# The first exponential's column moves into the identity's tile, and every later tile begins 1408 or 1376 bytes higher

## The chip, the cores and the metric

The kernel runs on one core of a Trainium2 chip. Its time is the device time of one execution in microseconds (us), and the figure shown is the median of three runs. Beside the runs stands one profiled execution, which the hardware profiler recorded instruction by instruction. The engines are called as the profile calls them: PE (TensorE's matmuls), PEld (TensorE's loads of the stationary operand), DVE (VectorE), ACT (ScalarE), POOL (GpSimd) and SP (SyncE, which issues nearly all transfers here).

## The reference

The reference computes an attention with a detour over 32 packed queries, and a feed-forward layer behind it, all in float32.

```python
def sm_attn(qq, kk, vv):                      # softmax attention, 8 batches, 8 heads
    s = scale * np.matmul(qq, kk.transpose(0, 1, 3, 2))
    a = np.exp(s - np.max(s, axis=-1, keepdims=True))
    a = a / (np.sum(a, axis=-1, keepdims=True) + 1e-09)
    return np.matmul(a, vv)
p_packed = sm_attn(p, k, v)                   # 32 packed rows from 576 tokens
out = sm_attn(q, p_packed, p_packed)          # 576 tokens from 32 packed rows
x = out.transpose(0, 2, 1, 3).reshape(4608, 512)
h = x @ w_in                                  # 512 -> 2048
g = h * (1.0 / (1.0 + np.exp(-h)))
return g @ w_out                              # 2048 -> 512
```

## The kernel before

The eight batches are worked through one after the other, with the attention of the next one laid between the feed-forward units of the present one. A unit is one batch and one block `f` of 128 of the 2048 hidden columns. For it, line 524 makes the hidden values (the product of the second softmax's shares `a2` with `pw`, which is the packed rows times `w_in`), lines 542 to 545 apply the activation, line 550 makes the remainder of the rounding, and line 560 adds the product with the rows of `w_out` to the sums in PSUM. To keep float32 accuracy on rounded operands, each product is made from three: upper by upper, upper by lower, lower by upper. So there are `g_hi` and `g_lo`, `wo_hi` and `wo_lo`, `pw_hi` and `pw_lo`, `a2_hi` and `a2_lo` (`a_hi` and `a_lo` in the profile).

In both lines the matmul has a stationary operand of 128 columns of 4 bytes (512 bytes in each partition), which PEld loads ahead, and a moving operand that PE streams. In line 560 the stationary operand is a block of `g` and the moving one a row of `w_out`, 512 columns or 2048 bytes. In line 524 the stationary one is a block of `pw` and the moving one is half of `a2`, 288 columns or 1152 bytes. The first few units (`u < WHOLE`) work on unrounded float32 with one product instead of three.

For PE, DVE, ACT and SP the order of the instructions is written out by hand: the string `ORDER` for the first two batches, `step_of` and the loop at the end for the others. Neither reads an address. At the start, POOL makes the identity (`make_identity`, line 112), ACT takes one exponential of its first column into `ready` (line 121), which brings the exponential's table in before it is needed, and PE multiplies the identity by itself (`keep_warm`, line 138, the step `W6`) until the first keys have landed (`k0`, line 144) and the first scores can start (`as0.0`, line 231). The framework finds out which instruction must wait for which from the tiles that they read and write.

Tiles in SBUF are laid out in the order of their pools and of their first use, one behind the other. `const` holds `ident`, `win`, `wo_hi`, `wo_lo`, `rest` and `ready`; behind it come `kvq`, `pw`, `a2p`, `tmp`, `small`, `gp`, `osb`, the staging buffers of the weights (`w_raw`) and, in the same place later, the third buffers of `pw` and `g`. A tile of `const` smaller than 32 bytes takes 32. In the program before, `ident` begins at byte 16512 of each partition, behind the framework's own 16384 + 128 bytes.

Of the kernel before, what the change touches and what calls it, by code (L numbers as in the profile page):

```python
# [9 lines left out]
F32 = mybir.dt.float32  # L10
# [9 lines left out]
P = 128  # L20
# [63 lines left out]
def packed_attention_ffn(ctx: ExitStack, tc: tile.TileContext, pkT, qT, v, w_in, w_out, out):  # L84
# [15 lines left out]
    const = ent(tc.tile_pool(name="const", bufs=1))  # L100
# [7 lines left out]
    ps_acc = ent(tc.tile_pool(name="ps_acc", bufs=2, space=PSUM))  # L108
    ps_two = ent(tc.tile_pool(name="ps_two", bufs=2, space=PSUM))

    ident = const.tile([P, P], F32, name="ident")
    make_identity(nc, ident)
    win = const.tile([P, NF, NI, P], I32, name="win")
    wo_hi = const.tile([P, NF, DM], F32R, name="wo_hi")
# [2 lines left out]
    rest = const.tile([P, NF, 2, 2, REST], F32, name="rest")  # L117
    parts = tc.dram_tile((EARLY, 2, P, 2, DM), F32, name="parts")

    ready = const.tile([P, 1], F32, name="ready")  # L120
    nc.scalar.activation(ready, ident[:, :1], AF.Exp)

    made = {}
# [663 lines left out]
```

## Time and profile before

| | |
|---|---|
| median of 3 runs | 717.23 us (717.07 to 717.65) |
| profiled execution, its own time | 716.94 us |
| its span, first to last instruction | 715.1 us |
| PE busy | 702.2 us, 98% of the span |
| DVE, ACT busy | 332.5 us, 328.7 us |

The span leaves out what lies before the first and behind the last instruction, 1.8 us here. PE's busy time counts a matmul until its end, and the matmuls of a row overlap one another, so the sum over groups is larger than the span and the spacing of starts says more than the durations. In the chain of waits, a piece is a stretch in which one line on one engine set the pace; its length divided by its count is the spacing of that line's matmuls.

### The profile page before, as it was taken

Reading aid. Unit: us, or ns where it says so; the run is one execution under the profiler, and the core shown is the slowest. Engines: PE = TensorE matmul, PEld = TensorE weight load, DVE = VectorE, ACT = ScalarE, POOL = GpSimd, SP = SyncE. Lnnn points to the kernel's source line nnn. Section 1 sums busy time; section 2 is a strip of 40 time slices with the busy share of each in tenths; the row PEclk is TensorE's granted clock in tenths of the full one; section 3 lists DMA queues with packets and bytes.
Section 4 is the critical chain, followed back from the end, with each engine's and each line's share of the span. In section 5 each row is a group of like instructions: output and inputs, shape, how many; then the busy total and the mean of one; then the engine's idle time right before and its main releaser. Section 6 shows DMA issues by size and latency. Waiting matters only on the chain.

```text
span 715.1 us, 12103 instructions
## 1 busy us (share of the span) xinstructions
PE 702.2 (98%) x5060; PEld 563.6 (79%) x5060; DVE 332.5 (46%) x491; ACT 328.7 (46%) x614; POOL 21.0 (3%) x16
## 2 busy tenths in 40 slices
PE   8999999999999999999999999999999999999997
PEld 5647778877778888878888788878878788788885
DVE  4989985944632346332542425432362333622112
ACT  4796858534535325362532625452343533533221
POOL 0202020200000000000000000000000000000000
PEclk9999999999999999999999999999999999999999
DMA  9765654405022130312112122112301210010002
GB/s 361 312 192 217 221 186 173 125 32 192 23 107 81 35 144 1 126 23 89 67 60 82 22 83 74 59 68 45 134 0 68 74 35 1 1 59 1 1 1 73
DMA packets 30869, 65.20 MB, mean 91 GB/s; under 512 B 19296, under 2 KB 19296, under 8 KB 26464
## 3 DMA queue, kind: packets, MB, share of 16 engines
q1 hardware_dynamic: 30720, 64.30, 25.9%
q8 instruction: 40, 0.66, 0.4%
q10 hardware_dynamic: 96, 0.13, 0.1%
q14 instruction: 13, 0.11, 0.0%
HBM read 48.76 MB, written 11.53 MB: 84 GB/s over the span
## 4 chain that ended last, share of the span: by engine, by line
PE 91%; DVE 4%; ACT 2%; DMA 1%; SPq 1%; issue 0%; ACTq 0%; DVEq 0%
PE ps_acc L560 56%; PE ps_two L524 27%; PE ps_two L231 6%; SPq L308 1%; PE ps_two L329 1%; DMA w_raw<-in_w_in 1%; DMA kvq_t<-in_pkT 1%; ACT tm L277 0%; PE ps_acc L231 0%; DVE win L204 0%; DVE mx L267 0%; DVE win L203 0%; PE ps_acc L329 0%; DVE tm L411 0%; DVE tm L434 0%
## 5 line engine op out<-in xcount | busy, mean ns | idle before, releaser
L560 PE MATMUL ps_acc<-wo_hi,g_hi 128*128 128x512 f32 x560 | 225.2, 402 | 0.0
L560 PE MATMUL ps_acc<-wo_hi,g_lo 128*128 128x512 f32 x560 | 221.5, 396 | 0.1
L560 PE MATMUL ps_acc<-wo_lo,g_hi 128*128 128x512 f32 x560 | 221.2, 395 | 0.0
L550 DVE TENSOR_TENSOR g_lo<-g,g_hi 128x512 fp32r<-128x512 f32 x124 | 89.3, 720 | 260.6 <-ACT g_hi L544 260.5
L542 ACT ACTIVATE g<-ps_two 128x512 f32<-128x512 f32 x124 | 74.4, 600 | 270.2 <-PE ps_two L524 241.1
L524 PE MATMUL ps_two<-a_lo,pw_hi 128*128 128x288 f32 x528 | 156.0, 304 | 0.1
L524 PE MATMUL ps_two<-a_hi,pw_hi 128*128 128x288 f32 x496 | 146.3, 295 | 1.0 <-ACT rest L545 1.0
L524 PE MATMUL ps_two<-a_hi,pw_lo 128*128 128x288 f32 x496 | 146.6, 296 | 0.0
L560 PEld LDWEIGHTS ps_acc<-wo_hi,g_hi 128*128 128x128 f32 x560 | 105.1, 188 | 40.1 <-issue 19.4
L560 PEld LDWEIGHTS ps_acc<-wo_hi,g_lo 128*128 128x128 f32 x560 | 105.2, 188 | 26.2 <-DVE g_lo L550 0.8
L560 PEld LDWEIGHTS ps_acc<-wo_lo,g_hi 128*128 128x128 f32 x560 | 105.2, 188 | 19.7
L524 PEld LDWEIGHTS ps_two<-a_lo,pw_hi 128*128 128x128 f32 x528 | 99.4, 189 | 7.4 <-ACT rest L545 0.8
L524 PEld LDWEIGHTS ps_two<-a_hi,pw_hi 128*128 128x128 f32 x496 | 93.1, 188 | 6.1 <-ACT rest L545 1.3
L524 PEld LDWEIGHTS ps_two<-a_hi,pw_lo 128*128 128x128 f32 x496 | 93.2, 188 | 0.0
L544 ACT ACTIVATE g_hi<-ps_two 128x512 fp32r<-128x512 f32 x124 | 73.7, 594 | 8.4 <-PE ps_acc L560 8.2
L492 DVE TENSOR_TENSOR pw_lo<-ps_two,pw_hi 128x1024 fp32r<-128x1024 f32 x31 | 36.8, 1220 | 10.0 <-ACT pw_hi L489 10.0
L489 ACT CAST pw_hi<-ps_two 128x1024 fp32r<-128x1024 f32 x31 | 30.1, 1015 | 16.7 <-PE ps_two L231 16.7
L231 PE MATMUL ps_two<-win,ppT 64*32 64x512 f32 (+1 forms) x560 | 32.7, 559 | 2.5 <-DVE pw_lo L492 1.6
L545 ACT ACTIVATE rest<-ps_two 128x64 f32<-128x64 f32 (+1 forms) x132 | 30.0, 228 | 0.0
L231 PEld LDWEIGHTS ps_two<-win,ppT 64*32 64x32 f32 x560 | 8.2, 105 | 18.0 <-issue 10.4
L542 ACT ACT_TABLE_LOAD x16 | 20.5, 1283 | 2.1 <-PE ps_two L524 1.9
L534 ACT CAST g_hi<-rest 128x512 fp32r<-128x512 f32 x16 | 9.9, 622 | 14.6 <-PE ps_acc L560 14.6
(116 smaller groups left out, 475.7 us busy)
## 6 DMA issues: line engine op xcount, KB each, us to landing
kvq_t<-in_v SPq DMA_DIRECT2D x8, 1280.0 KB, 6.4
kvq_t<-in_pkT SPq DMA_DIRECT2D x7, 1216.0 KB, 6.4
out<-o SPq DMA_DIRECT2D x16, 512.0 KB, 2.8
kvq_t<-in_qT SPq DMA_DIRECT2D x7, 1152.0 KB, 5.3
w_raw<-in_w_in SPq DMA_DIRECT2D x6, 1024.0 KB, 6.6
win<-in_w_out SPq DMA_DIRECT2D x3, 1024.0 KB, 5.5
w_raw<-in_w_out SPq DMA_DIRECT2D x3, 1024.0 KB, 4.7
tm<-tm SPq DMA_DIRECT2D x56, 40.0 KB, 2.0
```

Source lines behind the costliest of these rows:

```text
L231: nc.tensor.matmul(bank(par)[NP * i : NP * i + NP], lhs(r, i), rhs(r, i), start=True, stop=True)
L308: nc.sync.dma_start(self.e1T[NP * at : NP * at + NP, : some.shape[1], i], some)
L329: nc.tensor.matmul(self.ps[NP * i : NP * i + NP, par * D : par * D + D], e, vs[:n, c, h * D : h * D + D], start=(c == 0), stop=(c == 4),)
L489: nc.scalar.copy(self.hi, self.ps[:, :, : self.nf * P])
L492: nc.vector.tensor_tensor(self.lo, self.ps[:, :, : self.nf * P], self.hi.bitcast(F32), ALU.subtract)
L524: nc.tensor.matmul(bank, p[:, par, cols], a[:, par], start=(n == 0), stop=(n == len(todo) - 1))
L534: nc.scalar.copy(g_hi, g)
L542: nc.scalar.activation(g, ps[..., :MAIN], AF.Silu)
L544: nc.scalar.activation(g_hi, ps[..., :MAIN], AF.Silu)
L545: nc.scalar.activation(to, ps[..., MAIN:HS], AF.Silu)
L550: nc.vector.tensor_tensor(g_lo[:, c], g[:, c], g_hi[:, c].bitcast(F32), ALU.subtract)
L560: nc.tensor.matmul(bank, g[:, rows], w[:, at], start=(first and n == 0), stop=(last and n + 1 == len(todo)))
```

## The change

`ident` becomes a tile of 480 columns instead of 128, which is 1408 bytes longer. The program goes on using the first 128 columns under the name `ident`; column 128 is `ready`, and the other 351 are not used. The tile `ready` of its own goes away, with its 32 bytes.

```diff
-    ident = const.tile([P, P], F32, name="ident")
+    ident = const.tile([P, P + 352], F32, name="ident")
+    ready = ident[:, P : P + 1]
+    ident = ident[:, :P]
     make_identity(nc, ident)
 ...
-    ready = const.tile([P, 1], F32, name="ready")
     nc.scalar.activation(ready, ident[:, :1], AF.Exp)
```

No instruction is added or taken away, and no order is changed. `win`, `wo_hi`, `wo_lo` and `rest` begin 1408 bytes higher, and everything behind `const` begins 1376 bytes higher. By the sizes of the tiles, that moves the first bytes so:

| tile | before, modulo 2048 | modulo 512 | modulo 128 | after, modulo 2048 | modulo 512 | modulo 128 |
|---|---|---|---|---|---|---|
| `ident` | 128 | 128 | 0 | 128 | 128 | 0 |
| `win`, `wo_hi`, `wo_lo` (rows of 2048), `rest` | 640 | 128 | 0 | 0 | 0 | 0 |
| `kvq_t`, `pw` (blocks of 512), `tm` | 672 or 1696 | 160 | 32 | 0 or 1024 | 0 | 0 |
| `a2`, eight buffers of 2304, each in halves of 1152 | all different | 32, 160, 288, 416 | 32 | all different | 0, 128, 256, 384 | 0 |
| `g_hi`, `g_lo`, `g` (blocks of 512), `o`, `w_raw` | 1696 | 160 | 32 | 1024 | 0 | 0 |

The first byte of a moving `w_out` row and that of the stationary `g` block beside it differ by 32 bytes modulo 128 before, and by none after. Those of `a2` and `pw` differ by 0 modulo 128 before and after. The highest byte in use goes from 226976 to 228352.

## Prediction

> **What bounds the kernel now.** I read the page first: the engines' busy shares, the granted clock and the chain of waits.
>
> ```profile
> PE 702.2 (98%) x5060; PEld 563.6 (79%) x5060; DVE 332.5 (46%) x491; ACT 328.7 (46%) x614; POOL 21.0 (3%) x16
> PEclk9999999999999999999999999999999999999999
> PE 91%; DVE 4%; ACT 2%; DMA 1%; SPq 1%; issue 0%; ACTq 0%; DVEq 0%
> ```
>
> PE is busy in 98% of the span and is 91% of the chain, at the full granted clock throughout. What an address can change must therefore show in the pace of PE's matmuls; DVE, ACT and the transfers together hold some 7% of the chain. Next come the groups by line and form, for the counts.
>
> ```profile
> L560 PE MATMUL ps_acc<-wo_hi,g_hi 128*128 128x512 f32 x560 | 225.2, 402 | 0.0
> L560 PE MATMUL ps_acc<-wo_hi,g_lo 128*128 128x512 f32 x560 | 221.5, 396 | 0.1
> L560 PE MATMUL ps_acc<-wo_lo,g_hi 128*128 128x512 f32 x560 | 221.2, 395 | 0.0
> L524 PE MATMUL ps_two<-a_lo,pw_hi 128*128 128x288 f32 x528 | 156.0, 304 | 0.1
> L524 PE MATMUL ps_two<-a_hi,pw_hi 128*128 128x288 f32 x496 | 146.3, 295 | 1.0 <-ACT rest L545 1.0
> L524 PE MATMUL ps_two<-a_hi,pw_lo 128*128 128x288 f32 x496 | 146.6, 296 | 0.0
> ```
>
> Line 560 has 3 x 560 = 1680 rounded matmuls of 512 columns. Line 524 has 3 x 496 = 1488 of 288 columns, and 32 of the 528 are the unrounded ones of the first units. PE waits for almost nothing (the last column). The chain in order of time (start, length, what, count) gives the spacing of these matmuls.
>
> ```profile
> 0.74 3.81 DMA kvq_t<-in_pkT
> 52.60 6.78 DMA w_raw<-in_w_in
> ...
> 65.55 3.20 PE ps_two L524 x24
> ...
> 180.41 3.19 PE ps_two L524 x24
> ...
> 362.32 11.19 PE ps_acc L560 x48
> ...
> 531.56 11.19 PE ps_acc L560 x48
> ...
> 652.98 3.19 PE ps_two L524 x24
> 691.26 19.61 PE ps_acc L560 x84
> ```
>
> Line 560: 19.61/84 = 233.5 ns, 11.19/48 = 233.1 ns. Line 524: 3.19/24 = 132.9 ns. The spacing stays the same over 600 us, and it does not depend on what the other engines do, as the view by stretches shows (busy us and counts of PE, PEld, DVE, ACT, POOL, then clock, DMA share, GB/s).
>
> ```profile
> 151.20:154.10 2.90, 2.90 (x13) 2.35 (x14) 2.36 (x2) 1.14 (x2) 0.00 (x0) 1.00 0.02 6
> 362.40:373.40 11.00, 11.00 (x49) 8.82 (x48) 4.52 (x6) 4.55 (x8) 0.00 (x0) 1.00 0.26 97
> 695.00:710.00 15.00, 15.00 (x66) 12.00 (x66) 3.42 (x5) 2.88 (x4) 0.00 (x0) 1.00 0.19 70
> ```
>
> DVE is busy 41% of the second stretch (4.52 of 11.00) and 23% of the last (3.42 of 15.00), and the spacing is 233.1 against 233.5 ns. So traffic of DVE and ACT in SBUF does not set the pace; if addresses do, it is through PE's own two streams.
>
> **Is there anything to win in the pace?** The unrounded float32 matmuls of the first units have the same shapes, and a timeline of PE shows their spacing.
>
> ```profile
> 40.35 2.10 PE L524 MATMUL ps_two<-a_lo,pw_hi 128*128 128x288 f32 x8
> 42.29 1.88 PE L560 MATMUL ps_acc<-o,g_hi 128*128 128x512 f32 x4
> ```
>
> and the view of line 560 by itself has the time of one from start to end (least, median, most):
>
> ```profile
> L560 PE MATMUL ps_acc<-o,g_hi x32: 592/592/697, 34.3 to 58.3; 128*128 128x512 f32 x32
> ```
>
> Eight of 288 columns take 42.29 - 40.35 = 1.94 us, 242.5 ns each; four of 512 take (1.88 - 0.592)/3 = 429 ns. If such a record takes two clocks a column where a rounded one takes one, the rounded ones should take half: 214.5 and 121.3 ns. They take 233.5 and 132.9, so 19.0 and 11.6 ns are lost, in all 1680 x 19.0 + 1488 x 11.6 = 31.9 + 17.3 = 49.2 us. That is the most which any placement could give back; a gain beyond it is excluded.
>
> **Part by part.** *The column.* The exponential is the same instruction with another destination. The start of the timeline:
>
> ```profile
> 0.73 1.28 ACT L121 ACT_TABLE_LOAD   x1 [0.73 <-PEq L779]
> ...
> 1.36 2.63 PEld L138 LDWEIGHTS ps_two<-ident 128*128 128x128 f32 x12 [1.36 <-POOL ident masks.py:199]
> 1.36 2.93 PE L138 MATMUL ps_two<-ident 128*128 128x128 f32 x12 [1.36 <-POOL ident masks.py:199]
> ...
> 2.03 0.20 ACT L121 ACTIVATE ready<-ident 128x1 f32<-128x1 f32 x1
> ...
> 4.59 1.21 PE L231 MATMUL ps_acc<-kvq_t 64*32 64x288 f32 x16 [0.30 <-DMA kvq_t<-in_pkT]
> ```
>
> PE's twelve warming matmuls wait for POOL's identity and nothing else. If the framework took `ident` as a whole, they would now wait for ACT's write into column 128, to 2.03 + 0.20 = 2.23 instead of 1.36 us. Behind them on PE stand the first scores: the twelve end 2.93 us after their start, at 5.16 us, and the scores, at 4.59 now, would slip by at most 0.6 us; DVE's first maximum and ACT's first softmax wait for these. That is the upper end; the lower is 0. How the framework tells ranges of one tile apart can be seen on `win`:
>
> ```profile
> L231 PE MATMUL ps_two<-win,ppT x560: 266/589/613, 15.6 to 649.4; 64*32 64x512 f32 x165, 64*32 64x128 f32 x22
> L203 DVE TENSOR_SCALAR win<-w_raw x8: 408/686/690, 12.7 to 125.6; 128x1024 int32<-128x1024 int32 x6, 128x512 int32<-128x512 int32 x2
> ```
>
> PE reads the first blocks of `win` from 15.6 us, while DVE writes later ones until 125.6 us. Ranges are tracked, so I take 0.
>
> *The moving operands.* A row of `w_out` goes from 640 to 0 modulo 2048, but lies at 0 modulo 128 before and after. A half of `a2` goes from 32 to 0 modulo 128. What the 32 costs follows from the two shapes. The unrounded ones give (429 - 242.5)/224 = 0.833 ns a column and a fixed 2.7 ns. With that fixed part, line 560 takes (233.5 - 2.7)/512 = 0.451 ns a column, and line 524 should take 288 x 0.451 + 2.7 = 132.5 ns. It takes 132.9, so its worse start costs at most 0.4 ns, 0.6 us in 1488. Nor do larger steps matter: the eight buffers of `a2` stand at 32, 160, 288 and 416 modulo 512 and are taken in turn, and the pieces of 24 last 3.19 or 3.20 us at 65, 180 and 652 us alike. A cost by page of 512 or 2048 bytes would change with the buffer. I take 0 between 0 and -0.6 us.
>
> *The stationary operands.* A block of `g` or `pw` starts 32 bytes into 128 before, and at 0 after. No rounded matmul of before has an aligned one, so no row shows the price. If a load costs by the units of 128 bytes touched, it touches five before and four after. The lower end is that all 49.2 us come from the loads and a fifth goes, -9.8 us. The other end is that loads are hidden, which speaks from the groups:
>
> ```profile
> L560 PEld LDWEIGHTS ps_acc<-wo_hi,g_hi 128*128 128x128 f32 x560 | 105.1, 188 | 40.1 <-issue 19.4
> L524 PEld LDWEIGHTS ps_two<-a_hi,pw_lo 128*128 128x128 f32 x496 | 93.2, 188 | 0.0
> ```
>
> A load lasts 188 ns at both spacings, 233 and 133 ns. If loads were what costs 19.0 ns in line 560, the same load would cost 19.0 in line 524 too. The loss is 11.6 there, and 19.0/11.6 = 1.64 is nearer to the columns' 512/288 = 1.78 than to 1. The loss goes with what is streamed, so I take 0.
>
> [...]
>
> *The two streams together.* `w_out` and `g` differ by 32 modulo 128 before and by 0 after. `a2` and `pw` already differ by 0. Line 524 loses 11.6/288 = 0.0403 ns a column, line 560 19.0/512 = 0.0371. If the equal start made that difference, line 560 would lose 0.0032 x 512 = 1.6 ns more, 1680 x 1.6 = +2.7 us. The same difference is what a fixed part of some 2 to 3 ns makes, as worked out above, so I take 0.
>
> *Transfers.* All buffers now begin at multiples of 512.
>
> ```profile
> win<-in_w_out SPq DMA_DIRECT2D x3, 1024.0 KB, 5.5
> w_raw<-in_w_out SPq DMA_DIRECT2D x3, 1024.0 KB, 4.7
> ```
>
> `win` stood at 0 modulo 128 and `w_raw` at 32, and the better start is not faster for the same load. The chain holds 3.81 + 6.78 = 10.6 us of transfers; a tenth of that is 1.1 us. I take -0.1 us, of 0 to -1.1.
>
> [...]
>
> **Sum.** 0 (column) + 0 (moving) + 0 (stationary) + 0 (together) - 0.1 (transfers) = -0.1 us. The profiled execution took 716.94 us, 715.1 of span and 1.8 around it, 0.3 under the median, so 717.23 - 0.1 = 717.1 us.
>
> **Rivals.** *A. PE streams faster.* The loss is counted by units of 128 bytes that both streams touch. Line 560 goes from 16 + 5 = 21 to 20 units, 19.0/21 = 0.9 ns, x 1680 = 1.5 us; line 524 from 10 + 5 = 15 to 9 + 4 = 13, 11.6 x 2/15 = 1.55 ns, x 1488 = 2.3 us. Time: 717.2 - 3.8 = 713.4 us; with the whole fifth of the loads 707.4. For it: a real loss of 19.0 and 11.6 ns stands in every matmul, and what causes it is unknown. Against it: the ratio of the units is 21/15 = 1.4, that of the losses 1.64.
>
> *B. Slower: the streams meet.* Moving row and stationary block start on the same phase and stand in each other's way at once. Place: line 560, every matmul; price 1.6 ns, +2.7 us, 719.9 us. It decides as soon as the phase modulo 128 matters at all and 0 is the bad one; from 0.9 ns a matmul on (1.5 us) it could be measured. For it: line 524, in phase already, loses more a column. Against it: the fixed part explains that.
>
> *C. The column makes PE wait.* +0.6 us, 717.8 us, still unchanged; against it stands `win`.
>
> *D. The change doesn't do what it says*, because the layout rounds otherwise: 717.2 us. The sizes leave no room for it.
>
> **How the numbers follow.** My forecast 0.50, A 0.28, B 0.17, C 0.04, D 0.01. The measurement tells some 0.2%, 1.4 us, from no change. The forecast, C and D lie within it, but a little of the first may fall outside (transfers to -1.1 and moving to -0.6 together reach -1.7), and A and B begin there: faster 0.29, same 0.54, slower 0.17. The forecast's own range is 715.6 to 718.4. The range for 8 in 10 takes A's counted case and B's price: 712.5 to 720.4; beyond it lie the case of the loads (0.13) and a collision dearer than B's (0.07).
>
> **What would show it.** Right: pieces of 48 of line 560 again near 11.19 us and of 24 of line 524 near 3.19, the first PE matmul released by POOL's identity near 1.36 us, scores near 4.59. Rival A: a piece of 48 at 11.15 or less with PE's total shorter at equal counts. B: 11.27 or more. C: the first matmul at 2.23 us. My forecast is wrong as soon as the spacing of either line moves by more than 0.5 ns.

## The result, and the profile after

| | before | changed |
|---|---|---|
| median of the runs | 717.15 us (716.86 to 717.65) | 710.63 us (709.87 to 710.72) |
| ratio, with its 95% interval | | 0.9906 [0.9889, 0.9923] |
| span of the profiled execution | 715.1 us | 708.8 us |

The changed kernel is 0.94% faster, about 6.5 us. The lines of the program stand one further down: line 560 of before is 561, line 524 is 525. The groups by line and form (busy us, mean ns of one, idle before):

```profile
L561 PE MATMUL ps_acc<-wo_hi,g_hi 128*128 128x512 f32 x560 | 222.5, 397 | 0.0
L561 PE MATMUL ps_acc<-wo_lo,g_hi 128*128 128x512 f32 x560 | 219.0, 391 | 0.0
L561 PE MATMUL ps_acc<-wo_hi,g_lo 128*128 128x512 f32 x560 | 219.0, 391 | 0.1
L525 PE MATMUL ps_two<-a_lo,pw_hi 128*128 128x288 f32 x528 | 156.2, 305 | 0.2
L525 PE MATMUL ps_two<-a_hi,pw_hi 128*128 128x288 f32 x496 | 147.1, 297 | 1.0 <-ACT rest L546 1.0
L525 PE MATMUL ps_two<-a_hi,pw_lo 128*128 128x288 f32 x496 | 145.9, 294 | 0.0
...
L561 PEld LDWEIGHTS ps_acc<-wo_hi,g_hi 128*128 128x128 f32 x560 | 105.1, 188 | 38.7 <-issue 19.4 <-ACT o L607 0.5
```

The three groups of the `w_out` product lost 4 to 5 ns each (402, 395, 396 before), the three of the hidden values stayed (304, 295, 296), and a load still lasts 188 ns. The chain of waits shows the pace (start, length, what, count):

```profile
183.36 10.93 PE ps_acc L561 x48
...
360.16 10.95 PE ps_acc L561 x48
...
527.58 10.95 PE ps_acc L561 x48
...
647.57 3.19 PE ps_two L525 x24
685.41 19.09 PE ps_acc L561 x84
```

Pieces of 48 went from 11.19 to 10.95 us and the last piece of 84 from 19.61 to 19.09, which is 227.3 ns a matmul instead of 233.5. A piece of 24 of the other line is 3.19 us as before. From here on "sum 560" and "sum 524" are the sums of all times from the start of one rounded matmul of that line to the start of the next matmul, taken from the trace. Sum 560 went from 397.92 to 390.57 us, sum 524 from 200.4 to 200.7. So line 560 gave 7.4 us, and some 1 us went back in small amounts elsewhere (0.2 in line 524, 0.5 in line 231, 0.3 in the warming matmuls of line 138); the span is 6.3 us shorter. "Spacing" is the mean of these times without those that hold a wait (240 ns or more in line 560, 140 or more in line 524): 233.1 and 132.8 ns before, 228.6 and 132.9 after. Runs of one kernel lie up to 1.9 us apart (716.83 to 718.68 us for the kernel before, over all its runs), while the sums of kernels profiled more than once repeat to within 0.2 us. Small differences are therefore read from the sums.

The start of the timeline is what it was:

```profile
0.73 1.28 ACT L122 ACT_TABLE_LOAD   x1 [0.73 <-PEq L780]
...
1.36 2.93 PE L139 MATMUL ps_two<-ident 128*128 128x128 f32 x12 [1.36 <-POOL ident masks.py:199]
2.02 0.20 ACT L122 ACTIVATE ident<-ident 128x1 f32<-128x1 f32 x1
4.57 1.21 PE L232 MATMUL ps_acc<-kvq_t 64*32 64x288 f32 x16 [0.28 <-DMA kvq_t<-in_pkT]
```

The exponential writes into `ident`'s tile from 2.02 us on, and PE reads the identity from 1.36 us without waiting for it.

### The profile page after: what moved, and what is told of

Read it like the earlier page. It is cut to its first block, busy times and chain, and to the rows that moved or that the text cites. A ratio compares the mean times of both kernels' runs of the same rounds, so it can differ in the third digit from the quotient of the medians.

```text
span 708.8 us, 12103 instructions
## 1 busy us (share of the span) xinstructions
PE 696.7 (98%) x5060; PEld 564.7 (80%) x5060; DVE 332.4 (47%) x491; ACT 328.5 (46%) x614; POOL 21.0 (3%) x16
## 4 chain that ended last, share of the span: by engine, by line
PE 91%; DVE 5%; ACT 2%; issue 1%; DMA 1%; DVEq 0%; ACTq 0%
PE ps_acc L561 55%; PE ps_two L525 27%; PE ps_two L232 6%; PE ps_two L330 1%; DVE win L198 1%; DMA kvq_t<-in_pkT 1%; PE ps_acc L232 0%; ACT tm L278 0%; DVE win L204 0%; ACT w_raw L192 0%; ACT w_raw L193 0%; DVE w_raw L198 0%; ACT L543 0%; DVE win L197 0%; DVE win L205 0%
## 5 line engine op out<-in xcount | busy, mean ns | idle before, releaser
L561 PE MATMUL ps_acc<-wo_hi,g_hi 128*128 128x512 f32 x560 | 222.5, 397 | 0.0
L561 PE MATMUL ps_acc<-wo_lo,g_hi 128*128 128x512 f32 x560 | 219.0, 391 | 0.0
L561 PE MATMUL ps_acc<-wo_hi,g_lo 128*128 128x512 f32 x560 | 219.0, 391 | 0.1
```

Of the source, the lines that this page charges most:

```text
L561: nc.tensor.matmul(bank, g[:, rows], w[:, at], start=(first and n == 0), stop=(last and n + 1 == len(todo)))
```

## The experiments

Everything is in the pace of line 560, so the question was which address makes it: that of `g` (theory G, a rival's), that of `w_out`'s rows (theory W), or the distance between the two (theory R). "Distance" is the first byte of a `w_out` row less that of a `g` block, modulo 256. It is 224, or -32, before, and 0 in the changed kernel.

**w_out alone.** Rows at 0 modulo 2048 as in the changed kernel, everything behind the constants where it stood before, by a tile `ready` of its own that fills the gap; the distance becomes 96. Against the changed kernel:

```diff
-    ready = ident[:, P : P + 1]
+    ready = const.tile([P, 168], F32, name="ready")[:, :1]
```

> Rows of w_out begin at 0 modulo 2048 as in the changed kernel; everything behind the constants (g, pw, a2, the transfers' buffers) stands where it stood before, g's blocks at 160 modulo 512. Theory G (a stationary block of g that begins 32 bytes into 128 costs more to load): nothing is gained, 717.1 us, line 560 spaced 233 ns. Theory W (the moving row crosses a page boundary of 512 or 2048 bytes when it starts off one): the whole gain, 710.6 us, 228.6 ns. Theory R (only the distance of the two streams modulo 128 counts; 32 before, 0 changed): the distance is 96 here, not 0, so 717 us or at least not the full gain.

Measured: 718.75 us, ratio 1.0011 [1.0002, 1.0021]. Sum 560 is 398.3 us, spacing 233.4 ns. The chain:

```profile
533.19 11.20 PE ps_acc L561 x48
693.21 19.61 PE ps_acc L561 x84
```

The rows' alignment, the thing that the change names first, gained nothing by itself here. Theory W falls.

**g alone.** `w_out` where it stood before, everything behind the constants as in the changed kernel; the distance becomes 128.

```diff
-    ident = const.tile([P, P + 352], F32, name="ident")
-    ready = ident[:, P : P + 1]
+    ident = const.tile([P, P], F32, name="ident")
+    ready = const.tile([P, 352], F32, name="ready")[:, :1]
```

> The mirror of the run with w_out alone: w_out's rows stay at 640 modulo 2048 (128 modulo 512), everything behind the constants stands as in the changed kernel, g's blocks at 0 modulo 512. Theory G: the whole gain, 710.6 us, 228.6 ns. Theory W: none, 717.1 us, 233 ns. Theory R: the distance is 0 modulo 128, so the whole gain, 710.6 us; if the distance counts modulo 512 (it is 128), less.

Measured: 716.60 us, ratio 0.9986 [0.9977, 0.9996], sum 560 397.0 us.

```profile
531.18 11.15 PE ps_acc L561 x48
690.74 19.54 PE ps_acc L561 x84
```

The time is 1.1 us below that of the kernel before beside it, about a sixth of the gain, and line 560 gives 0.9 us of its 7.4. Theory G falls, and with it a distance that counts modulo 128: the sum at 128 is 397.0 us, at 0 390.6.

**Both 512 bytes higher, and both 32 bytes higher.** The identity's tile has 608 and 488 columns instead of 480; the distance stays 0.

> The changed kernel with everything behind the identity 512 bytes higher: rows of w_out at 512 modulo 2048, g's blocks at 0 modulo 512. If the 2048 matters (theory W with a page of 2048 bytes), the gain is lost, 717 us and 233 ns. Theories G, R and W with pages of 512: unchanged from the changed kernel, 710.6 us, 228.6 ns.

> The changed kernel with everything behind the identity 32 bytes higher: both w_out and g begin at 32 modulo 128, their distance stays 0. Theory R: the gain stays, 710.6 us, 228.6 ns. Theory G: lost, since g straddles again, 717 us, 233 ns. Theory W: lost as well, 717 us.

Measured, one execution each: 709.78 and 710.17 us; sum 560 390.6 and 390.7 us; spacing 228.6 and 228.7 ns. The chain of the one with 32 bytes:

```profile
527.14 10.97 PE ps_acc L561 x48
685.00 19.11 PE ps_acc L561 x84
```

Here both operands begin 32 bytes off a multiple of 64, and the gain is whole.

**Thirty-two bytes.** The kernel before, with the column in the identity's tile but only 8 columns more. `w_out` moves by 32 bytes (with `win` and `rest` beside it), and everything from `kvq` on stands exactly where it stood before.

```diff
-    ident = const.tile([P, P + 352], F32, name="ident")
+    ident = const.tile([P, 136], F32, name="ident")
```

> The kernel before, with the exponential's column in the identity's tile but that tile only 32 bytes longer. w_out's rows then begin at 672 modulo 2048, and everything from the keys' buffers on stands exactly where it stood before, g's blocks at 160 modulo 512: nothing is aligned to 64, 128, 512 or 2048, but w_out and g both stand at 160 modulo 512, a distance of 0. Theory R (the distance of the two streams modulo 512 decides, alignment does not): the whole gain, 710.6 us, line 560 spaced 228.6 ns. Theory G or W (alignment of one of them): 717.1 us, 233 ns.

Measured: 710.23 us, ratio 0.9897 [0.9881, 0.9914], sum 560 390.5 us.

```profile
526.87 10.93 PE ps_acc L561 x48
684.67 19.09 PE ps_acc L561 x84
```

The whole gain comes without one buffer behind the constants being moved and with nothing aligned. Theory R is what is left; the runs further down that move one operand of line 560 alone exclude that it is `win` or `rest`.

**The distance by steps.** In the kernel before, the tile `ready` of its own gets 64, 112 or 56 columns, which sets the distance to 256, 64 and 32.

> The kernel before with the exponential's own tile 256 bytes long: w_out at 128 modulo 512, g at 384, a distance of 256 modulo 512. If the period of theory R is 256 bytes, the distance counts as 0: 710.6 us, 228.6 ns. If it is 512: no gain by it or another amount, 715 to 718 us, 231 to 234 ns.

> The kernel before with the exponential's own tile 448 bytes long: w_out at 128, g at 64 modulo 512, a distance of +64. Theory R with a window around 0 as wide as a row of 64 bytes or more: 710.6 us, 228.6 ns. With a narrow window (0 alone): 716 to 718 us, 232 to 234 ns.

> The kernel before with the exponential's own tile 224 bytes long: w_out at 128, g at 96 modulo 256, a distance of +32, where the kernel before has -32. If the distance counts symmetrically around 0, it is as slow as before, 717 us and 233 ns for line 560. If what counts is whether the load runs ahead of or behind the streamed row, a positive one behaves like +64 or better: 709 to 713 us, 227 to 230 ns.

With the runs above, by distance (the times of e3, e4, e6, e7 and e9 are single executions; before stood between 716.8 and 718.7 us beside all of them):

| distance modulo 256 | runs | sum 560, us | time, us |
|---|---|---|---|
| 0 | changed; e3, e4, e5; e6 (256) | 390.6; 390.6, 390.7, 390.5; 390.5 | 710.6; 709.8, 710.2, 710.2; 709.75 |
| 32 | e9 | 398.1 | 718.05 |
| 64 | e7 | 392.7 | 713.0 |
| 96 | e1 | 398.3 | 718.75 |
| 128 | e2 | 397.0 | 716.6 |
| 224 | before | 397.9 | 717.15 |

A distance of 256 gave what 0 gave (390.5 us against 390.5 to 390.7), and 128 did not (397.0): among the steps tried, a period of 256 bytes fits. It isn't a matter of ahead or behind: +32 was as bad as -32 (398.1 and 397.9 us). At 64 most of the gain is there (392.7 us), a case between the two that were expected of e7. 160 and 192, and steps finer than 32, were not tried.

**One operand of three.** The kernel with 32 bytes, and 128 bytes more distance for `g_lo` alone (its tile longer by 64 columns, used from column 32 on), or for `wo_lo` alone, by the same means. What lies behind these tiles moves by multiples of 256 bytes, which leaves every other distance as it was.

```diff
-            g_lo = pool.tile([P, 512], F32R, name="g_lo")
+            g_lo = pool.tile([P, 576], F32R, name="g_lo")[:, 32:544]
 ...
-    wo_lo = const.tile([P, NF, DM], F32R, name="wo_lo")
+    wo_lo = const.tile([P, NF * DM + 64], F32R, name="wo_lo")[:, 32 : 32 + NF * DM].rearrange("p (f e) -> p f e", e=DM)
```

> The kernel with the 32 bytes alone, and only the blocks of g_lo moved by 128 modulo 256 against w_out; g_hi stays at a distance of 0. If a load disturbs the matmul that runs while it is loaded, the spacing behind the matmul of wo_lo with g_hi grows (from 228.8 to some 232 ns), since g_lo is loaded under it, and the one behind wo_hi with g_lo does not: about 712.5 us. If a matmul is disturbed by the place of its own stationary operand, it is the spacing behind wo_hi with g_lo that grows. If g's place has nothing to do with it, neither grows: 710.2 us.

> The kernel with the 32 bytes alone, and only wo_lo's rows 128 bytes further on modulo 256; wo_hi, g_hi and g_lo keep their distance of 0. Only the matmul of wo_lo with g_hi streams at another distance. If the disturbance ends with the matmul whose stream stands wrong, the spacing behind wo_lo grows alone, from 228.8 to 232 to 236 ns, and the two others stay at 228.5: 712 to 713 us. If a disturbed matmul throws the next load out of step, the spacing behind wo_hi with g_lo grows too, as it did with g_lo moved: 714 to 716 us.

Measured: 715.18 and 715.83 us. Spacing behind each of the three matmuls, ns:

| | `wo_hi` with `g_hi` | `wo_lo` with `g_hi` | `wo_hi` with `g_lo` |
|---|---|---|---|
| 32 bytes alone (e5) | 228.4 | 228.8 | 228.6 |
| `g_lo` moved (e10) | 229.5 | 232.3 | 233.4 |
| `wo_lo` moved (e12) | 233.0 | 233.4 | 229.2 |

In the trace of the changed kernel, the load of the next stationary operand starts 2 to 4 ns after the running matmul starts (1613 of the 1712 loads of line 561), so `g_lo` is loaded while `wo_lo` streams. With `g_lo` moved, that spacing grew, from 228.8 to 232.3 ns, as expected of a disturbance by the load, but the one behind `wo_hi` with `g_lo`, during which the well-placed `g_hi` is loaded, grew too, from 228.6 to 233.4, which none of the three expected cases had. With `wo_lo` moved, it was not the spacing behind `wo_hi` with `g_lo` that grew beside its own, as I had expected, but the one behind `wo_hi` with `g_hi`. Of its 139 groups of twelve most repeat 236, 234, 230 ns (in the order of the table), and 22, at the same distances in bytes, repeat 226, 234, 226. All 22 have a pause behind their first matmul (334 or 335 ns); none of the 104 groups without such a pause has that pattern. In it only the matmul with the wrong distance is slow; in the other one its neighbours are longer too, 236 and 230 ns instead of 226. So the pair with the wrong distance has 234 ns in both patterns, and what its neighbours have depends on what went before. To which of the two loads around a matmul the distance counts is not settled: e10 alone would fit its own load or the next one.

**The other line.** Line 524 has the same kind of pair, `a2` streamed and `pw` loaded. The two halves of an `a2` buffer lie 1152 bytes apart, so one half stands at 0 and the other at 128 modulo 256 from `pw`, in every version so far. In the following, each half has 1280 bytes, so both stand alike; the second to fourth also move `a2` by 32, 64 and 128 bytes in its buffer (o = 0, 8, 16, 32). `a2_hi` and the unrounded `a2` are treated likewise. Line 560 stays at a distance of 0.

```diff
-            lo = a2p.tile([P, 2, HS], F32R, name="a2_lo")
+            lo = a2p.tile([P, 2, HS + 32], F32R, name="a2_lo")[:, :, o : o + HS]
```

> The kernel with the 32 bytes alone, and each half of a2 given 1280 bytes instead of 1152, so that both halves of every buffer stand at 0 or 256 modulo 512 from pw's blocks, where before the second halves stood at 128 or 384. If theory R holds for line 524 as for line 560, line 524 gets faster than 132.9 ns, to some 129.5 ns (4.5 of 233 ns is 1.9%, or 2 to 4 ns), 706 us. If line 524's 288 columns have no better distance: 132.9 ns and 710.6 us.

> The kernel with both halves of a2 at one distance from pw, and that distance +32 instead of 0 modulo 256; line 560 at a distance of 0. If line 524 answers to the distance as line 560 does, its spacing moves from 131.5 ns, by the same sign as line 560 at +32 against 0; if line 524 has only the two states of equal and unequal halves, it stays at 131.5 ns and 709.5 us.

> Both halves of a2 at a distance of +64 from pw, line 560 at 0. At +64 line 560 stood between its best and its worst. If line 524 does likewise: 131.5 to 133 ns. If line 560's first matmuls follow from where the last a2 row stood against g, its spacing is 227.3 ns as with +32, and the time 706 to 709 us; if not, 229.6 as with 0, and 709 to 711 us.

> Both halves of a2 at a distance of 128 from pw, the far point of a period of 256. If line 524 answers as line 560: its worst, some 134 ns, 711 us. If only equal halves count: 131.5 ns, 709 us.

| distance of `a2` from `pw` | run | sum 524, us | sum 560, us | time, us |
|---|---|---|---|---|
| 0 and 128 | changed | 200.7 | 390.6 | 710.6 |
| 0 | e8 | 198.6 | 392.3 | 709.5 |
| 32 | e11 | 201.2 | 388.4 | 708.6 |
| 64 | e13 | 199.0 | 390.6 | 708.3 |
| 128 | e14 | 201.4 | 389.4 | 710.25 |

Line 524 answered by the same signs, 0 and 64 good (198.6 and 199.0 us), 32 and 128 bad (201.2 and 201.4), but by 2.8 us in all where line 560 gave 7.8. Its spacing is 131.5, 133.4, 131.8 and 133.5 ns in the order of the rows; at 0 it falls short of the 129.5 ns that were expected. Its chain at a distance of 0:

```profile
613.93 3.16 PE ps_two L525 x24
646.41 3.16 PE ps_two L525 x24
684.34 19.13 PE ps_acc L561 x84
```

What e8 and e11 brought up unforeseen is the last column but one: line 560 changed with `a2`, by up to 3.9 us (392.3 to 388.4). (With `a2` at 64 its spacing is 228.6 ns, neither of the two values expected.) The trace shows where. Within a group of twelve its spacings settle at 226 and 227 ns, and the first ones after line 524 are longer: 228, 235, 233, 236, 224, 231, 236, 228, 233, 231 ns with `a2` at 0, and mostly 226 or 227 from the first on with `a2` at 32. So the first spacings of line 560 differed with the place of `a2` in line 524 before them, with `a2` at 0 for ten matmuls.

**A layout that beats both.** The one at 32 was timed by itself, and then with the one at 64 and the changed kernel on one chip.

> The same kernel as the run with a2 at +32, timed. It is expected to beat the changed kernel: 708.6 us against 710.6, line 560 at 227.3 ns and line 524 at 133.4 ns. If its one time was chance, 709.5 to 710.7 us.

> The changed kernel again, timed in more rounds on the chip on which the two layouts of a2 run: 710.6 us, ratio 0.990.

> The kernel with w_out and g at a distance of 0 and both halves of a2 at +64 from pw: 708.3 us by its one time, ratio 0.988. If it beats the changed kernel, its interval lies below the changed kernel's.

> The same with both halves of a2 at +32: 708.8 us, ratio 0.988. It should differ from the one at +64 by less than 0.5 us, since line 560 gains there (227.3 against 228.6 ns) what line 524 loses (133.4 against 131.8 ns).

| | time, us | ratio to before | sum 560 | sum 524 |
|---|---|---|---|---|
| changed (f1) | 709.83 (709.64 to 711.48) | 0.9894 [0.9877, 0.9910] | 390.7 | 200.7 |
| `a2` at 64 (f2) | 708.13 (708.09 to 709.69) | 0.9876 [0.9862, 0.9891] | 390.7 | 199.0 |
| `a2` at 32 (f3) | 708.29 (708.19 to 708.41) | 0.9873 [0.9859, 0.9888] | 388.5 | 201.2 |

The one timed by itself (e15) had 708.78 us, ratio 0.9882 [0.9866, 0.9899]. Both beat the kernel before clearly. Against the changed kernel, every run of `a2` at 32 lies below the changed kernel's fastest, by 1.2 us at the least, while the intervals of the ratios still overlap: probably some 1.5 us faster, and not more than that is claimed.

## Why the prediction was wrong

The forecast was 717.1 us and no change; the time was 710.6, below the range. By its steps:

- **The two streams together.** This is the step that failed. I saw that `w_out` and `g` stood 32 bytes apart modulo 128 and would stand at 0, and set it to 0, with +2.7 us as the bound. It is worth -7.4 us in line 560. Two errors lay behind it. The period that the runs fit is 256 bytes (e6: 390.5 us) and not 128 (e2: 397.0 us). And I took line 524 as a sample of a pair that is already in phase, which made phase 0 look like the worse one; half of its matmuls stood at 128, the slower place in the later runs, so its loss a column mixed good and bad: its spacing was 132.8 ns, with all its matmuls at 0 it is 131.5 (e8), with all at 128 it is 133.5 (e14).
- **The moving operands, larger steps.** From equal pieces of 24 I concluded that steps of 128 to 384 bytes don't matter. Every such piece holds both halves of `a2` in equal number, and its buffers differ by multiples of 256, a step that changed nothing in line 560 (e6: 390.5 us). The comparison could not have shown the effect. That a fixed part of 2.7 ns and one price a column joined the two lines to within 0.4 ns was chance: with both lines at 0 the same working gives (227.3 - 2.7) x 288/512 + 2.7 = 129.0 ns for line 524, and e8 has 131.5. That the row's own start costs nothing held in these runs: e1 moves it alone and gains nothing (ratio 1.0011), and e4 takes the alignment away and loses nothing (sum 560 390.7 us).
- **The stationary operands.** Nothing by themselves, as forecast: e2 gains 0.9 us of line 560's sum, at a distance that differs as well. The argument that the loss goes with the columns (1.64 against 1.78) and so cannot come from the loads was wrong, since both losses held a part that changed with the distance: a load lasts 188 ns before and after, and line 560 is spaced 233.1 ns before and 228.6 after. That a load is hidden was not borne out either: with only the loaded `g_lo` moved by 128 bytes, the mean spacing of line 560 rises from 228.6 ns (e5) to 231.7 (e10); no run shows why. Against the supposed 214.5 and 121.3 ns, the loss with both lines at 0 is 227.3 - 214.5 = 12.8 ns in line 560 and 131.5 - 121.3 = 10.2 in line 524, a ratio of 1.25. That is nearer to 1 than to 1.78, but it doesn't show what costs them.
- **The column and the transfers.** The column was right. The 0.1 us of the transfers was an estimate of mine that no run shows, and it is too little to be seen here. PE starts at 1.36 us, released by POOL, and the scores at 4.57 us. The chain's first transfer takes 3.79 us instead of 3.81, and the 1024 KB of `w_out` into `w_raw` 4.8 us from issue to landing instead of 4.7. The 6.78 us of `w_raw` at 52.6 us are not among the longest pieces any more; what that was worth cannot be told apart from the 1 us that went the other way.
- **The rivals.** A had the sign and the place, PE's matmuls, and a time of 713.4 us, but by another mechanism: units touched by each operand on its own. Against it speak e2, which takes one of A's units from every load and gives 0.9 us in line 560 and none in line 524 (pieces of 24 at 3.19 us, as before), and e4 and e5, in which both operands straddle and the gain is whole (sum 560 390.7 and 390.5 us); e1 changes none of the units that A counts. The case of the loads, with 707.4 us and a chance of 0.13, lay on the side of the range where the time came out, but e4 excludes it as the cause: that was no merit of the forecast. B, streams that meet, named the right thing, the place of the one operand to the other, with the wrong sign: equal phase was the good one (390.5 to 390.7 us in line 560, against 397.9 before). C and D did not happen.
- **The bound.** The 49.2 us were counted as the most that a placement could give back. They rest on the supposition that a rounded matmul can take half the time of an unrounded one, which no run shows: at a distance of 0 the two lines have 227.3 of 429 ns (0.53) and 131.5 of 242.5 (0.54). The best layout gave 9.6 us (717.72 to 708.13). What makes the 12 to 13 ns a matmul that line 560 stays above the supposed half, and the some 10 of line 524, is open.

## What to carry to other kernels

Where PE is the bound with rounded float32 and a new stationary operand for every matmul, the distance between the streamed operand and the loaded one modulo 256 is worth trying out like a tile size: it gave 1% here, it took no more memory than 32 bytes moved from one tile to another (e5), and it can change unasked whenever a small tile is added ahead of the large ones. That other kernels respond alike was not tried. Aligning the rows of `w_out` by themselves gained nothing here (e1, ratio 1.0011), though aligning all tensors to 256 bytes sets the distance to 0 as a by-product. A comparison within a trace says something about an address only if its samples differ in that address; list them by the candidate period before concluding that it has no effect.

## What the runs showed of the hardware that I had not expected

- In these runs the rounded float32 matmuls of 512 columns were spaced between 226.7 ns (settled, distance 0) and about 233.5 ns (mean, distances 32, 96 and 224) by the distance of their two operands in SBUF, at a granted clock of 1.00 in the stretches looked at before and after.
- The spacing depended on what went before: the same distances in bytes ran in different steady patterns (236, 234, 230 or 226, 234, 226 ns in e12, the second only behind a pause), and with `a2` at 0 (e8) the first ten matmuls of line 560 behind line 524 differed from the settled 226 and 227 ns by up to 10.
- Before the change the settled spacings alternate, 231 or 232 and 235 ns; after it they are 226 or 227. The alternation stood in the trace before the change and was lost in the means; the distance is 224 there and 0 in the changed kernel.
